# A reordered prologue in a sparse-attention and cosine-MLP kernel

## The chip, the cores and the metric

The kernel runs on one core of one Trainium2 chip. The metric is device time of one execution in microseconds (us). Engines: TensorE (PE, with its weight loads PEld), VectorE (DVE), ScalarE (ACT), GpSimd (POOL) and SyncE (SP), which here only issues transfers.

## The reference

```python
# q, k, v: (8 batches, 8 heads, 576 positions, 64)
scores = q @ k.T / sqrt(64)
mask_local   = (rel >= 0) & (rel < 32)                  # heads 0 to 3; rel = row - column
mask_strided = (rel >= 0) & (row % 32 == column % 32)   # heads 4 to 7
attn = softmax(where(mask, scores, -1e9)) @ v
x = attn, heads side by side                             # (4608 tokens, 512)
h = x @ w_in                                             # w_in: 512 x 2048
out = (h * cos(h)) @ w_out                               # w_out: 2048 x 512
```

The weights arrive as 64-bit floats, in pairs of 32-bit words, and the kernel makes float32 of them itself.

## The kernel before, in words

**Stages.** For each batch, attention gives x, transposed (features on partitions, 576 tokens in the free dimension). A first phase multiplies x by w_in and writes h to memory; a last phase reads h back, computes h*cos(h) and multiplies by w_out. Nearly all of this is matmuls on PE. Every large product is made of three: an operand is split into a high part (a cast, `x_hi` or `w` on ACT) and a remainder (a subtraction on POOL or DVE, `x_lo` and the second half of `w`), and PE adds high by high, high by low and low by high.

**Attention in units.** A batch has four strided units and three local ones. A unit loads q, k and v, gets its mask and its scores into a PSUM bank (L229, then L337 or L285), and goes through a softmax: DVE takes the maximum (L244) and subtracts it (L245), ACT makes the exponential (L250), DVE sums (L252), adds a tiny constant (L253) and takes the reciprocal (L254), POOL multiplies (L256). A strided unit is then turned by PE (L350), copied to SBUF by ACT (L354), multiplied by v (L363) and copied to x by ACT (L371, L377); once all four are there, x is split (`FirstOperands.split`, L155 on ACT and L156 on POOL, two halves of 288 tokens each). A local unit is turned by DVE (L293), multiplied by v (L303) and split straight from PSUM (L316 on ACT, L317 on DVE). So of the 512 features 256 are strided and 256 are local.

**Weights.** `land` brings 512 KB of w_in into one of three `raw` buffers; `to_float32` takes two operations of ACT (L142, L146) and two of DVE (L147, L150); `split` is a cast on ACT (L155) and a subtraction on POOL (L156). Two such pieces make the weights of one block `f` of 256 output columns; there are eight blocks.

**The prologue.** `PROLOGUE` says which unit takes its next step at which stage, and `BUSY` how many products of a zero tile (`keep_busy`, L630) PE makes after the scores of each stage. At stage 6 the conversion of the first two pieces of weights is put in, with the split of strided x. After the prologue comes the first batch, `FirstBlock`: eight products (L468) for each block, numbered n = 4*half + 2*rows + features, where features 0 are the strided ones and 1 the local ones. `FIRST` takes them in the order 0 to 7, so each PSUM bank gets its strided product and then its local one. Batch 1's scores and later attention work stand between these products, and the operations of all engines are placed by a scheduler that keeps each engine's queue in one fixed order, so an instruction waits for all that stand ahead of it on its engine.

**Later.** From batch 1 on a block has seven products of sums of operands (L497), for which POOL makes sums of weights (L182 to L192) and splits of x during the end of the first batch.

Of the kernel before, what the change touches and what calls it, by code (L numbers as in the profile page):

```python
# [26 lines left out]
P = 128  # L27
# [12 lines left out]
SU = 6  # L40
# [20 lines left out]
FIRST = ((0,), (1,), (2,), (3,), (4,), (5, 6), (7,))  # L61
PER_BATCH = NF * STEP
# [7 lines left out]
PROLOGUE = ((0,), (1,), (0, 2), (0, 1, 3), (1, 2, 4), (2, 3, 5), (3, 6), (4, 4), (5, 5), (6, 6))  # L70
BUSY = (10, 6, 5, 4, 4, 4, 4, 3, 3, 3)
# [9 lines left out]
def attention_cos_ffn(ctx, tc, qkl, vl, qkvs, w_in, w_out, eye, eye16, mask_l0, mask_l, mask_s, out):  # L81
# [15 lines left out]
    warm = const.tile([P, 64], BF16, name="warm")  # L97
# [101 lines left out]
    class Attention:  # L199
        def __init__(self, stack):  # L200
# [9 lines left out]
            self.kept, self.x = None, {}  # L210
# [7 lines left out]
        def pe(self, mm):  # L218
            return mm if self.plain else in_turn(mm)
# [5 lines left out]
        def score_bank(self, b, mask):  # L225
# [8 lines left out]
            if self.kept is None:  # L234
                self.kept = self.bank(self.scores)
                nc.vector.memset(self.kept, 0.0)
# [29 lines left out]
        def inputs(self, b, n):  # L266
            if b == 0:
                t = wp.tile([P, 6 * 2 * P], F32, name="v")
                return t[:, :n], t[:, n:]
            qk = self.ld.tile([P, max(QKL, QS + KS)], F32, name="qk")  # L270
            return qk, self.ld.tile([P, max(VL, VS)], F32, name="v")
# [53 lines left out]
        def strided(self, b, p, u):  # L325
            real = min(SU, NG - SU * u)
            qk, v = self.inputs(b, QS + KS)
            loads.append(nc.sync.dma_start(out=qk[:, :QS + KS], in_=qkvs[b, p, u, :, :QS + KS]))
# [16 lines left out]
            pn = next(self.pn_s)  # L345
# [106 lines left out]
    class FirstBlock:  # L452


        def __init__(self, f):
            self.f = f

        def products(self, slot):
            for n in FIRST[slot]:
                j, i, k = n // 4, n // 2 % 2, n % 2  # L460
                (wh, wl), (xh, xl) = wi[self.f][2 * i + k], operands[0].made[2 * k + j]
                if k == 0:
                    self.bank = pools["m"].tile([P, 512], F32, name="m")[:, :TH]
# [3 lines left out]
                for m, (a, y, c) in enumerate(ops):  # L467
                    in_turn(nc.tensor.matmul(  # L468
                        self.bank, a[:, c * P:(c + 1) * P], y[:, c], start=k == 0 and m == 0,
                        stop=k == 1 and m == len(ops) - 1, skip_group_check=True,  # L470
                    ))
                if k == 1:
                    h = getattr(self, f"h{i}")
                    if i:
                        nc.vector.tensor_copy(out=h[:, TH * j:TH * (j + 1)], in_=self.bank)
                    else:
                        nc.scalar.copy(out=h[:, TH * j:TH * (j + 1)], in_=self.bank)
# [124 lines left out]
    with ExitStack() as phase:  # L602
# [19 lines left out]
        att.banks(True, (m,), (o,), (acc[1], acc[2]), (m,))  # L622
# [5 lines left out]
        def keep_busy(n, after):  # L628
            for _ in range(n):
                mm = nc.tensor.matmul(  # L630
                    spare[:64], warm, warm.unsqueeze(1).broadcast_to([P, 8, 64]), start=True, stop=True
# [6 lines left out]
        for k, staged in enumerate(PROLOGUE):  # L638
# [4 lines left out]
            if k == 6:  # L643
                for i in range(2):
                    list(input_weights(cv, 0, i))
                operands[0].split(0)
# [178 lines left out]
```

## Time and profile before

| what | value |
|---|---|
| median of 3 runs | 890.8 us (887.82 to 892.25) |
| the profiled execution | 890.38 us, of which the span is 888.6 us |
| PE busy | 880.3 us, 99% of the span |
| DVE, ACT, POOL busy | 569.6, 531.0, 396.9 us |
| mean granted clock of PE | 0.995 |

The span is what the hardware profiler recorded, and 1.8 us of the execution lie around it. Matmuls are pipelined and overlap in the records, so PE reads as busy while it waits between small matmuls; the chain of waits and the start times say more than its busy share. A granted clock of 1.00 is 2.4 GHz, 0.50 is 1.2 GHz.

### The profile page before, as it was taken

The numbers are of one execution on the slowest core, as the hardware profiler recorded it, in microseconds if no ns is written. First come the engines' busy times: TensorE is split into PE (matmuls) and PEld (weight loads), VectorE is DVE, ScalarE is ACT, GpSimd is POOL, SyncE is SP. The second block draws the span as 40 slices with busy tenths as digits, with TensorE's granted clock in tenths as the row PEclk, the third lists the DMA queues.
The fourth block names the chain that finished last, engine by engine and source line by source line (L and its number), as shares of the span: only waits on it lengthen the run. The fifth ranks groups of instructions, "written<-read, shape, count | busy, mean of one in ns | idle before, by whom it ended". The sixth has DMA issues, their size and how long they took to land.

```text
span 888.6 us, 21381 instructions
## 1 busy us (share of the span) xinstructions
PE 880.3 (99%) x8453; PEld 780.9 (88%) x8453; DVE 569.6 (64%) x967; ACT 531.0 (60%) x1020; POOL 396.9 (45%) x337
## 2 busy tenths in 40 slices
PE   9999999999999999999999999999999999999998
PEld 5899999999999999999999888888888888888886
DVE  4788756757567676676425666666666666666662
ACT  3666544545345454454456777777777777777772
POOL 2568984415115051151455444444444444444442
PEclk9899999999999999999999999999999999999999
DMA  9488444565656556643285434343444344443431
GB/s 329 157 297 269 155 163 157 190 214 176 203 183 243 195 182 211 204 159 125 104 269 194 125 98 150 96 142 110 128 117 128 113 128 115 123 123 115 132 106 47
DMA packets 70516, 143.83 MB, mean 162 GB/s; under 512 B 8208, under 2 KB 15632, under 8 KB 70416
## 3 DMA queue, kind: packets, MB, share of 16 engines
q1 hardware_dynamic: 69696, 142.24, 50.0%
q8 instruction: 66, 1.08, 0.5%
q14 instruction: 34, 0.28, 0.1%
q10 hardware_dynamic: 720, 0.23, 0.1%
HBM read 91.06 MB, written 51.38 MB: 160 GB/s over the span
## 4 chain that ended last, share of the span: by engine, by line
PE 89%; POOL 3%; DVE 2%; DMA 2%; ACT 2%; issue 2%; SPq 0%; ACTq 0%; POOLq 0%
PE acc L588 45%; PE m L497 18%; PE n L497 9%; PE m L468 5%; PE o L497 4%; PE acc L303 2%; PE acc L285 2%; PE acc L363 2%; POOL x_lo L156 1%; PE acc L337 1%; DMA raw<-in_w_in 1%; PE acc L350 1%; DMA both<-w_all 1%; DMA v<-in_qkvs 0%; POOL v L156 0%
## 5 line engine op out<-in xcount | busy, mean ns | idle before, releaser
L156 POOL TENSOR_TENSOR g_lo<-r,g_hi 128x512 fp32r<-128x512 f32 x144 | 187.2, 1300 | 207.9 <-ACT g_hi L155 199.3
L588 PE MATMUL acc<-w,g_hi 128*128 128x512 f32 x720 | 223.1, 391 | 0.0
L577 DVE TENSOR_TENSOR r<-r,h_in 128x512 f32<-128x512 f32 x144 | 153.0, 1062 | 103.2 <-ACT r L573 103.1
L588 PEld LDWEIGHTS acc<-w,g_hi 128*128 128x128 f32 x720 | 135.3, 188 | 28.5
L588 PE MATMUL acc<-w,g_lo 128*128 128x512 f32 x360 | 141.1, 392 | 0.0
L571 ACT ACTIVATE r<-h_in 128x512 int32<-128x512 f32 x144 | 91.2, 633 | 80.5 <-POOL g_lo L156 80.3
L588 PE MATMUL acc<-v,g_hi 128*128 128x512 f32 x432 | 133.9, 391 | 0.0
L573 ACT ACTIVATE r<-r,quarter 128x512 f32<-128x512 f32 x144 | 104.3, 724 | 20.6 <-DVE r L572 15.9
L572 DVE SCALAR_TENSOR_TENSOR r<-r,h_in 128x512 f32<-128x512 int32 x144 | 101.7, 706 | 22.0 <-ACT r L571 13.2
L497 PE MATMUL m<-x_hi,w 128*128 128x288 f32 x448 | 109.8, 300 | 1.7 <-DVE h L515 1.6
L497 PE MATMUL m<-x_hi,v 128*128 128x288 f32 x448 | 108.9, 298 | 0.1
L588 PEld LDWEIGHTS acc<-v,g_hi 128*128 128x128 f32 x432 | 81.0, 188 | 17.2 <-ACT h L513 0.2
L155 ACT CAST g_hi<-r 128x512 fp32r<-128x512 f32 x144 | 89.6, 622 | 4.0 <-PE acc L588 1.8
L588 PE MATMUL acc<-v,g_lo 128*128 128x512 f32 x216 | 84.7, 392 | 0.0
L588 PEld LDWEIGHTS acc<-w,g_lo 128*128 128x128 f32 x360 | 67.6, 188 | 15.8
L497 PEld LDWEIGHTS m<-x_hi,w 128*128 128x128 f32 x448 | 78.0, 188 | 3.3 <-DVE h L515 2.4
L497 PEld LDWEIGHTS m<-x_hi,v 128*128 128x128 f32 x448 | 78.0, 188 | 1.2 <-ACT m L505 0.4
L505 ACT COPY m<-m 128x288 f32<-128x288 f32 x112 | 44.4, 397 | 55.2 <-PE m L497 51.1
L256 POOL TENSOR_TENSOR pn_s<-e_sb,z 128x324 f32<-128x324 f32 x32 | 23.3, 729 | 102.5 <-DVE z L254 77.8
L497 PE MATMUL m<-x_lo,w 128*128 128x288 f32 x224 | 66.1, 295 | 0.0
L497 PE MATMUL m<-x_lo,v 128*128 128x288 f32 x224 | 66.1, 295 | 0.0
L256 POOL TENSOR_TENSOR e_sb<-e_sb,z 128x384 f32<-128x384 f32 x24 | 20.4, 851 | 85.8 <-DVE z L254 76.2
(111 smaller groups left out, 1720.2 us busy)
## 6 DMA issues: line engine op xcount, KB each, us to landing
h_all<-h SPq DMA_DIRECT2D x128, 288.0 KB, 2.7
h_in<-h_all SPq DMA_DIRECT2D x144, 256.0 KB, 2.7
out<-o SPq DMA_DIRECT2D x36, 256.0 KB, 2.5
qk<-in_qkvs SPq DMA_DIRECT2D x28, 324.0 KB, 4.2
qk<-in_qkl SPq DMA_DIRECT2D x21, 416.0 KB, 4.0
raw<-in_w_in SPq DMA_DIRECT2D x16, 512.0 KB, 5.2
raw<-in_w_out SPq DMA_DIRECT2D x16, 512.0 KB, 4.5
v<-in_vl SPq DMA_DIRECT2D x24, 224.0 KB, 3.1
```

What stands on the lines that cost most here:

```text
L155: with_product(nc.scalar.copy(out=hi, in_=x))
L156: nc.gpsimd.tensor_tensor(out=lo, in0=x, in1=hi.bitcast(F32), op=ALU.subtract)
L256: nc.gpsimd.tensor_tensor(out=pn, in0=e, in1=z[:, :n].unsqueeze(2).broadcast_to([P, n, w]), op=ALU.mult)
L285: self.scored = self.pe(nc.tensor.matmul(s_ps[quarter_of(c), t * KW:(t + 1) * KW], q_t[half(j), p, QB * t:QB * (t + 1)], k_t[half(j), p, Q ...
L468: in_turn(nc.tensor.matmul(self.bank, a[:, c * P:(c + 1) * P], y[:, c], start=k == 0 and m == 0, stop=k == 1 and m == len(ops) - 1, skip_g ...
L497: in_turn(nc.tensor.matmul(bank, a[:, c * P:(c + 1) * P], y[:, c], start=first and i == 0, stop=i == len(ops) - 1, skip_group_check=True,))
L505: nc.scalar.copy(out=t, in_=self.bank[name[0]])
L571: with_product(nc.scalar.activation(out=k, in_=h, func=AF.Copy, scale=1.0 / (2.0 * math.pi), bias=0.25))
L572: nc.vector.scalar_tensor_tensor(out=r, in0=k, scalar=-2.0 * math.pi, in1=h, op0=ALU.mult, op1=ALU.add)
L573: sin = nc.scalar.activation(out=r, in_=r, func=AF.Sin, bias=quarter)
L577: nc.vector.tensor_tensor(out=r, in0=r, in1=h, op=ALU.mult)
L588: in_turn(nc.tensor.matmul(acc[t], g[:, at], w, start=(f == 0 and i == 0), stop=(f == NFC - 1 and i == 2)))
```

## The change

The edits: (1) in `PROLOGUE` the first step (scores and softmax) of each unit keeps its stage, and the later steps of the strided units come two stages later (those of the last one three and five), so that the local units' scores have less ahead of them; (2) `BUSY` now has 9 zero products at the start and 2 after each of six scores, 21 in place of 46, and each has 128 weight columns in place of 64; (3) weight conversion is put behind the scores of stage 6 (`turn = att.scored`), the split of strided x behind stage 9; (4) the four strided units of batch 0 no longer share the two `pn_s` tiles but write their probabilities into the unused end of their input tile, which POOL clears; (5) the second bank of a local unit's product comes from `acc0` and no longer from the three `m` banks; (6) the first block takes its eight products in the order of `VERY_FIRST`, three strided ones first, and keeps several banks open; (7) the scores' bank from batch 1 on is cleared by a zero product on PE and not by DVE.

```diff
@@ -59,6 +59,8 @@
 STEP = 7
 FIRST = ((0,), (1,), (2,), (3,), (4,), (5, 6), (7,))
+
+VERY_FIRST = ((0, 2), (4,), (1,), (3,), (5,), (6,), (7,))
 PER_BATCH = NF * STEP
 EXTRA = 2
@@ -67,8 +69,8 @@
 UNITS = 7
 KNOTS = ((UNITS, 1), (2 * UNITS + 2, PER_BATCH - 8), (B * UNITS + 2, (B - 1) * PER_BATCH - 8))
-PROLOGUE = ((0,), (1,), (0, 2), (0, 1, 3), (1, 2, 4), (2, 3, 5), (3, 6), (4, 4), (5, 5), (6, 6))
-BUSY = (10, 6, 5, 4, 4, 4, 4, 3, 3, 3)
+PROLOGUE = ((0,), (1,), (2,), (3,), (0, 4), (1, 0, 5), (2, 1, 6), (3, 2), (4, 4), (3,), (5, 5), (6, 6))
+BUSY = (9, 2, 2, 2, 2, 2, 2)
 TB = 512
 NTB = NTOK // TB
@@ -94,7 +96,7 @@
         nc.scalar.dma_start(out=t, in_=src)
     quarter = const.tile([P, 1], F32, name="quarter")
     nc.vector.memset(quarter, math.pi / 2.0)
-    warm = const.tile([P, 64], BF16, name="warm")
+    warm = const.tile([P, P], BF16, name="warm")
     nc.vector.memset(warm, 0.0)
     h_all = dram.tile([NFC, P, NTOK], F32, name="h_all")
     w_all = dram.tile([NFC, P, DM], F32, name="w_all")
@@ -207,7 +209,7 @@
             for t in pn_s:
                 nc.gpsimd.memset(t, 0.0)
             self.pn_s = itertools.cycle(pn_s)
-            self.kept, self.x = None, {}
+            self.kept, self.spare, self.x = None, None, {}
         def banks(self, plain, scores, transposed, products, second):
             self.plain = plain
@@ -216,6 +218,7 @@
             )
         def pe(self, mm):
+            self.last = mm
             return mm if self.plain else in_turn(mm)
         def bank(self, kind):
@@ -233,7 +236,9 @@
                 return bank
             if self.kept is None:
                 self.kept = self.bank(self.scores)
-                nc.vector.memset(self.kept, 0.0)
+                in_turn(nc.tensor.matmul(
+                    self.kept, warm, warm.unsqueeze(1).broadcast_to([P, 4, P]), start=True, stop=True
+                ))
             return self.kept
         def softmax(self, b, s, mask, n, w, pn=None):
@@ -266,6 +271,7 @@
         def inputs(self, b, n):
             if b == 0:
                 t = wp.tile([P, 6 * 2 * P], F32, name="v")
+                self.spare = t[:, 6 * 2 * P - SU * GP:].rearrange("p (t k) -> p t k", k=GP)
                 return t[:, :n], t[:, n:]
             qk = self.ld.tile([P, max(QKL, QS + KS)], F32, name="qk")
             return qk, self.ld.tile([P, max(VL, VS)], F32, name="v")
@@ -325,6 +331,7 @@
         def strided(self, b, p, u):
             real = min(SU, NG - SU * u)
             qk, v = self.inputs(b, QS + KS)
+            spare = self.spare
             loads.append(nc.sync.dma_start(out=qk[:, :QS + KS], in_=qkvs[b, p, u, :, :QS + KS]))
             nc.sync.dma_start(out=v[:, :real * D], in_=qkvs[b, p, u, :, QS + KS:QS + KS + real * D])
             q_t = qk[:, :QS].rearrange("p (t q) -> p t q", q=GB)
@@ -342,7 +349,11 @@
             yield [
                 partial(score, t, i) for t in range(SU) for i in range(2) if SU * u + t // 2 * 2 + i < NG
             ], "64x64"
-            pn = next(self.pn_s)
+            if b == 0:
+                pn = spare
+                nc.gpsimd.memset(pn, 0.0)
+            else:
+                pn = next(self.pn_s)
             self.softmax(b, s_ps[:, :SU * GB].rearrange("p (t w) -> p t w", w=GB), mask, SU, GB, pn[:, :, :GB])
             yield
             t_ps = self.bank(self.transposed)
@@ -453,28 +464,28 @@
         def __init__(self, f):
-            self.f = f
+            self.f, self.banks = f, {}
         def products(self, slot):
-            for n in FIRST[slot]:
+            for n in (FIRST if self.f else VERY_FIRST)[slot]:
                 j, i, k = n // 4, n // 2 % 2, n % 2
                 (wh, wl), (xh, xl) = wi[self.f][2 * i + k], operands[0].made[2 * k + j]
                 if k == 0:
-                    self.bank = pools["m"].tile([P, 512], F32, name="m")[:, :TH]
+                    self.banks[i, j] = pools["m"].tile([P, 512], F32, name="m")[:, :TH]
                     if j == 0:
                         setattr(self, f"h{i}", hb.tile([P, S], F32, name="h"))
                 ops = [(a, y, c) for c in range(2) for a, y in ((wh, xh), (wh, xl), (wl, xh))]
                 for m, (a, y, c) in enumerate(ops):
                     in_turn(nc.tensor.matmul(
-                        self.bank, a[:, c * P:(c + 1) * P], y[:, c], start=k == 0 and m == 0,
+                        self.banks[i, j], a[:, c * P:(c + 1) * P], y[:, c], start=k == 0 and m == 0,
                         stop=k == 1 and m == len(ops) - 1, skip_group_check=True,
                     ))
                 if k == 1:
                     h = getattr(self, f"h{i}")
                     if i:
-                        nc.vector.tensor_copy(out=h[:, TH * j:TH * (j + 1)], in_=self.bank)
+                        nc.vector.tensor_copy(out=h[:, TH * j:TH * (j + 1)], in_=self.banks[i, j])
                     else:
-                        nc.scalar.copy(out=h[:, TH * j:TH * (j + 1)], in_=self.bank)
+                        nc.scalar.copy(out=h[:, TH * j:TH * (j + 1)], in_=self.banks[i, j])
                     if j == 1:
                         nc.sync.dma_start(out=h_all[2 * self.f + i, :, :S], in_=h)
@@ -619,7 +630,7 @@
         att = Attention(attention)
         m, n, o = ((pools[name], name) for name in "mno")
         acc = [(ps, f"acc{i}") for i in range(3)]
-        att.banks(True, (m,), (o,), (acc[1], acc[2]), (m,))
+        att.banks(True, (m,), (o,), (acc[1], acc[2]), (acc[0],))
         operands[0] = FirstOperands()
         units = [unit for b in range(B) for unit in att.units(b)]
@@ -628,7 +639,7 @@
         def keep_busy(n, after):
             for _ in range(n):
                 mm = nc.tensor.matmul(
-                    spare[:64], warm, warm.unsqueeze(1).broadcast_to([P, 8, 64]), start=True, stop=True
+                    spare, warm, warm.unsqueeze(1).broadcast_to([P, 4, P]), start=True, stop=True
                 )
                 if after is not None:
                     order(mm, after, "in its place")
@@ -641,8 +652,11 @@
             if k + 1 < len(BUSY):
                 keep_busy(BUSY[k + 1], att.scored)
             if k == 6:
+                turn = att.scored
                 for i in range(2):
                     list(input_weights(cv, 0, i))
+            if k == 9:
+                turn = att.last
                 operands[0].split(0)
                 operands[0].split(1)
         for i in range(2):
```

**PE, where the products begin.** These rows are of PE around the scores of the first unit of batch 1 (`acc0_...<-qk`). `m_...` are the banks of the first block, `x_hi_119`, `x_hi_121` the two halves of strided x, `x_hi_123`, `x_hi_125` those of local x (`x_lo` likewise), `pt_l` the turned probabilities of a local unit. Before:

```order
L303 MATMUL m_574<-pt_l_469,v_430 64x32 x2
L468 MATMUL m_628<-x_hi_119,w_482 128x288
L468 MATMUL m_628<-x_lo_120,w_482 128x288
L468 MATMUL m_628<-x_hi_119,w_482 128x288 x2
L468 MATMUL m_628<-x_lo_120,w_482 128x288
L468 MATMUL m_628<-x_hi_119,w_482 128x288
L468 MATMUL m_628<-x_hi_123,w_482 128x288
L468 MATMUL m_628<-x_lo_124,w_482 128x288
L468 MATMUL m_628<-x_hi_123,w_482 128x288 x2
L468 MATMUL m_628<-x_lo_124,w_482 128x288
L468 MATMUL m_628<-x_hi_123,w_482 128x288
L337 MATMUL acc0_653<-qk_649 54x54 x12
```

After the change:

```order
L479 MATMUL m_629<-x_hi_121,w_434 128x288
L479 MATMUL m_629<-x_lo_122,w_434 128x288
L479 MATMUL m_629<-x_hi_121,w_434 128x288 x2
L479 MATMUL m_629<-x_lo_122,w_434 128x288
L309 MATMUL acc0_553<-pt_l_424,v_385 64x32 x2
L309 MATMUL acc0_553<-pt_l_424,v_385 64x64 x10
L309 MATMUL acc0_553<-pt_l_424,v_385 64x32 x2
L479 MATMUL m_629<-x_hi_121,w_434 128x288
L239 LDWEIGHTS warm_75
L239 MATMUL acc0_640<-warm_75 128x512
L344 MATMUL acc0_640<-qk_636 54x54 x12
L479 MATMUL m_607<-x_hi_123,w_434 128x288
```

Before, all products of the local units (L303) stand ahead of the first large product, and the first bank takes strided and local x in a row. In the changed kernel three products of strided x stand here, the last local unit's second product (L309) is inside the third of them, and local x is read only behind batch 1's first scores.

**ACT, the middle of the prologue.** `raw_...` to `n_...` and `w_...` are the steps of the weights, `e_sb` the exponential of a unit (324 wide strided, 384 local), `pt` and `x0` the copies of strided units. Before:

```order
L371 COPY x0_251<-acc1_238 128x6x18x3
L354 COPY pt_257<-o_253 128x324
L142 ACTIVATE n_477<-raw_474 128x512
L146 ACTIVATE raw_474<-raw_474 128x512
L146 ACTIVATE raw_485<-raw_485 128x512
L250 ACTIVATE e_sb_336<-e_sb_336 128x384
L371 COPY x0_251<-acc2_288 128x4x18x3
L377 COPY x0_251<-acc2_288 128x18x2
L155 CAST w_482<-v_476 128x512
L142 ACTIVATE n_487<-raw_485 128x512
L354 COPY pt_305<-o_301 128x324
L146 ACTIVATE raw_607<-raw_607 128x512
```

After the change:

```order
L255 ACTIVATE e_sb_352<-e_sb_352 128x384
L144 ACTIVATE n_429<-raw_426 128x512
L382 COPY x0_321<-acc2_372 128x4x18x3
L388 COPY x0_321<-acc2_372 128x18x2
L148 ACTIVATE raw_426<-raw_426 128x512
L148 ACTIVATE raw_437<-raw_437 128x512
L365 COPY pt_451<-o_447 128x324
L255 ACTIVATE e_sb_414<-e_sb_414 128x384
L382 COPY x0_321<-acc1_453 128x6x18x3
L157 CAST w_434<-v_428 128x512
L144 ACTIVATE n_439<-raw_437 128x512
L148 ACTIVATE raw_586<-raw_586 128x512
```

The first conversion (L142, now L144) stood behind the fourth unit's exponential and ahead of the first local unit's; now it stands behind the second local unit's.

**POOL, the splits.** `w_...` are the splits of weights, `x_lo_120` and `x_lo_122` those of strided x, `e_sb` the multiplication of the local units. Before:

```order
L156 TENSOR_TENSOR w_482<-v_476,w_482 128x512
L256 TENSOR_TENSOR e_sb_336<-e_sb_336,z_341 128x384
L156 TENSOR_TENSOR w_492<-v_476,w_492 128x512
L256 TENSOR_TENSOR e_sb_401<-e_sb_401,z_406 128x384
L156 TENSOR_TENSOR w_615<-v_609,w_615 128x512
L256 TENSOR_TENSOR e_sb_459<-e_sb_459,z_464 128x384
L156 TENSOR_TENSOR x_lo_120<-x0_251,x_hi_119 128x576
L156 TENSOR_TENSOR x_lo_122<-x0_251,x_hi_121 128x576
L156 TENSOR_TENSOR w_625<-v_609,w_625 128x512
L156 TENSOR_TENSOR w_699<-v_678,w_699 128x512
```

After the change:

```order
L261 TENSOR_TENSOR e_sb_288<-e_sb_288,z_293 128x384
L261 TENSOR_TENSOR e_sb_352<-e_sb_352,z_357 128x384
L158 TENSOR_TENSOR w_434<-v_428,w_434 128x512
L261 TENSOR_TENSOR e_sb_414<-e_sb_414,z_419 128x384
L158 TENSOR_TENSOR x_lo_120<-x0_321,x_hi_119 128x576
L158 TENSOR_TENSOR x_lo_122<-x0_321,x_hi_121 128x576
L158 TENSOR_TENSOR w_444<-v_428,w_444 128x512
L158 TENSOR_TENSOR w_594<-v_588,w_594 128x512
L158 TENSOR_TENSOR w_604<-v_588,w_604 128x512
L158 TENSOR_TENSOR w_685<-v_665,w_685 128x512
```

Before, three pieces of weights were split ahead of strided x; now one is, and the second piece, which the second product of the changed order reads, comes behind both splits of x.

## Rows read from the trace of the kernel before

**Rows 1.** The page, its first part (busy time, share of the span and instructions of each engine) and the granted clock in 40 slices of 22 us.

```profile
PE 880.3 (99%) x8453; PEld 780.9 (88%) x8453; DVE 569.6 (64%) x967; ACT 531.0 (60%) x1020; POOL 396.9 (45%) x337
...
PEclk9899999999999999999999999999999999999999
```

**Rows 2.** The chain that ended last, in order of time: start in us, length in us, what.

```profile
9.77 8.11 DMA raw<-in_w_in
...
29.80 1.20 PE acc L303 x28
...
34.12 3.18 PE m L468 x12
37.30 0.74 PE acc L337 x24
38.04 4.99 PE m L468 x36
```

**Rows 3.** Windows of 1 us: busy time of PE, PEld, DVE, ACT and POOL with instructions, granted clock, DMA share, GB/s.

```profile
30.00:31.00 1.00, 1.00 (x29) 0.94 (x26) 0.80 (x2) 1.00 (x3) 1.00 (x3) 0.73 0.58 229
31.00:32.00 1.00, 1.00 (x5) 0.19 (x6) 0.97 (x3) 1.00 (x5) 1.00 (x1) 0.50 0.30 45
...
37.00:38.00 1.00, 1.00 (x27) 0.71 (x25) 0.00 (x0) 0.67 (x2) 0.00 (x0) 0.86 0.00 0
38.00:39.00 1.00, 1.00 (x9) 1.00 (x8) 0.91 (x2) 0.85 (x2) 0.00 (x0) 1.00 0.06 16
```

**Rows 4.** Zero products: their group in the first 40 us (count, busy us, mean ns, idle before), from the view of groups by form.

```profile
L630 PE MATMUL acc<-warm 128*64 128x512 bf16 x46 | 14.2, 449 | 1.0 <-DVE warm L98 1.0
```

**Rows 5.** Zero products in the timeline of PE: start, length, line, count.

```profile
0.99 4.47 PE L630 MATMUL acc<-warm 128*64 128x512 bf16 x10 [0.99 <-DVE warm L98]
...
6.86 1.48 PE L630 MATMUL acc<-warm 128*64 128x512 bf16 x6
```

**Rows 6.** The timeline of DVE in the prologue: start, length, and in brackets the idle time ahead with what ended it.

```profile
6.98 0.49 DVE L244 TENSOR_REDUCE mx<-m 128x6 f32<-128x324 f32 x1 [6.04 <-PE m L337]
...
17.57 0.56 DVE L244 TENSOR_REDUCE mx<-m 128x6 f32<-128x384 f32 x1 [1.33 <-PE m L285]
...
28.92 0.19 DVE L254 RECIPROCAL z<-z 128x6 f32<-128x6 f32 x1
29.41 0.70 DVE L147 SCALAR_TENSOR_TENSOR n<-raw,n 128x512 int32<-128x512 int32 x1 [0.30 <-ACT n L142]
```

**Rows 7.** The timeline of ACT, same columns.

```profile
17.90 0.63 ACT L142 ACTIVATE n<-raw 128x512 int32<-128x512 uint32 x1 [0.39 <-DMA raw<-in_w_in]
18.47 1.40 ACT L146 ACTIVATE raw<-raw 128x512 f32<-128x512 f32 x2
...
20.18 0.35 ACT L371 COPY x<-acc 128x216 f32<-128x216 f32 x1
20.42 0.18 ACT L377 COPY x<-acc 128x36 f32<-128x36 f32 x1
...
22.02 0.68 ACT L146 ACTIVATE raw<-raw 128x512 f32<-128x512 f32 x1
22.98 0.52 ACT L250 ACTIVATE e_sb<-e_sb 128x384 f32<-128x384 f32 x1 [0.28 <-DVE e_sb L245]
23.57 0.62 ACT L155 CAST w<-v 128x512 fp32r<-128x512 f32 x1
24.09 0.64 ACT L142 ACTIVATE n<-raw 128x512 int32<-128x512 uint32 x1
24.66 0.48 ACT L371 COPY x<-acc 128x324 f32<-128x324 f32 x1
25.02 0.43 ACT L354 COPY pt<-o 128x324 f32<-128x324 f32 x1
...
29.78 1.25 ACT L155 CAST x_hi<-x 128x576 fp32r<-128x576 f32 x2
30.93 0.31 ACT L316 CAST x_hi<-acc 128x192 fp32r<-128x192 f32 x1
...
32.45 0.25 ACT L316 CAST x_hi<-acc 128x96 fp32r<-128x96 f32 x1
...
37.34 0.40 ACT L477 COPY h<-m 128x288 f32<-128x288 f32 x1 [1.49 <-PE m L468]
```

**Rows 8.** The timeline of POOL, same columns.

```profile
30.95 2.79 POOL L156 TENSOR_TENSOR x_lo<-x,x_hi 128x576 fp32r<-128x576 f32 x2
33.70 1.27 POOL L156 TENSOR_TENSOR w<-v,w 128x512 fp32r<-128x512 f32 x1
39.91 1.30 POOL L156 TENSOR_TENSOR w<-v,w 128x512 fp32r<-128x512 f32 x1 [4.94 <-ACT w L155]
```

**Rows 9.** Longer windows, columns as in rows 3.

```profile
40.00:60.00 20.00, 20.00 (x247) 19.29 (x245) 16.57 (x39) 13.23 (x28) 12.14 (x13) 1.00 0.85 280
60.00:80.00 20.00, 20.00 (x337) 19.00 (x339) 16.26 (x32) 13.70 (x30) 16.31 (x17) 1.00 0.83 262
80.00:95.00 15.00, 15.00 (x304) 14.38 (x297) 10.96 (x27) 7.75 (x18) 13.77 (x16) 1.00 0.74 256
95.00:112.00 17.00, 16.40 (x197) 15.71 (x197) 13.77 (x25) 8.82 (x21) 17.00 (x15) 1.00 0.42 137
```

**Rows 10.** DMA issues of the first 45 us by line: count, KB each, median us from issue to landing.

```profile
raw<-in_w_in SPq DMA_DIRECT2D x9, 512.0 KB, 5.3
```

## The prediction

> **What bounds the kernel now.** First the page's totals: PE is busy for 880.3 of the 888.6 us of the span [rows 1], so only what frees PE, or starts its large products sooner, moves the end. Then the chain of waits, in order of time: up to 34 us it runs through transfers, ACT and DVE, and from 34.12 on through the large products L468 without a gap (12 in 3.18 us, scores in 0.74, 36 in 4.99) [rows 2]. The order shows that PE's queue behind the first block's first 30 products is unchanged. So the change acts on the first 34 us, and the question is how much earlier PE gets through its first large products, and whether that lead survives. Third, the granted clock, us by us: PE falls from 2.4 to 1.2 GHz between 30 and 31 us, while small local products run, and is back at 2.4 between 37 and 38 [rows 3]. At the low level a large product takes 3.18/12 = 0.265 us, at the high one 4.99/36 = 0.139 [rows 2].
>
> A point that both kernels reach is needed. I take "18 large products and batch 1's first scores done". Before it is 38.04 + 6 x 0.139 = 38.87 us [rows 2].
>
> **The change part by part.**
>
> *Fewer zero products.* Before there are 46 with 14.2 us of busy time [rows 4], at 4.47/10 = 0.45 us on the low clock and 1.48/6 = 0.25 on the high one [rows 5]. 25 go: 1 x 0.45 + 24 x 0.25 = 6.4 us of PE. This is no gain in itself: DVE waits for PE only at times there (1.33 us ahead of the first local unit [rows 6]), and the head is set by what comes next. The 64 more weight columns I cost at nothing (a zero product streams 512 columns either way; at most its 0.25 again, twice per unit, in time that PE spends waiting).
>
> *Local softmax sooner, weights behind it.* DVE has to pass three times over each strided unit (0.49) and four times over each local one (0.56): 4 x 3 x 0.49 + 3 x 4 x 0.56 = 12.6 us, and 14 small operations of 0.19, 2.7: from 6.98 that ends at 22.3 if DVE never waits; before, the last reciprocal stood at 28.92 [rows 6], because conversions of weights stood in between and PE's scores came late. So DVE is no longer what is last; ACT is. Its order after the change can be added up from the arrival of the first piece of weights, which nothing in the change moves (its transfer ends the 8.11 us of [rows 2], and L142 starts at 17.90 [rows 7]). Up to the first `x_hi` of strided x stand, with durations from [rows 7]: L142 0.63, copies 0.35 + 0.18, L146 twice 1.40, copy of pt 0.43, exponential 0.52, copy of x 0.48, cast of w 0.62, L142 0.64, L146 0.68, two local `x_hi` 0.62, copies 0.35 + 0.18, and the cast itself 0.62: 7.70 us, so 25.6. Before, that cast ended at 29.78 + 0.62 = 30.4 [rows 7]. POOL then makes both `x_lo`, 2.79, and only then the low part of the second piece of weights, 1.27 [rows 8], which the third matmul of the second product reads: 29.7 us.
>
> Both sides of this: starts on ACT follow each other by about 0.1 less than the durations (23.57 to 24.09 for a cast of 0.62 [rows 7]), 13 times: 28.4 at the earliest. And ACT can be a microsecond late at the start, if DVE's share takes the 1.33 us of waiting that it had at 17.57 [rows 6]: 30.7 at the latest.
>
> *Strided products at the head.* From 29.7 on stand the last four matmuls of the second product and five of the third, up to the last local unit's second product: at the low clock 9 x 0.265 = 2.39, so 32.1. That local product also needs its bank back, thus the splits of the second local unit, which the new order puts behind conversions on ACT and DVE: after 25.6 ACT has the second `x_hi` 0.62, a cast 0.62, L142 0.64, L146 0.68, two small `x_hi` 0.50, a cast 0.62, L142 0.62, two more 0.50 = 4.80 [rows 7], so 30.4, and DVE in between two passes of 0.70 [rows 6] and a split of about 0.25: 32.1, the same. Then 1.20 for the local product at a falling clock (28 matmuls [rows 2]), 0.27 for the last of the 18, 0.45 for the zero product that replaces DVE's clearing, 0.74 for the scores: **34.8**, against 38.87: **4.1 us sooner**. The low end of the waits (1.3 less, all at the high clock, where the bank is the later one at 30.8) gives 30.8 + 0.6 + 0.14 + 0.25 + 0.74 = 32.5, 6.4 sooner. The high end (30.7 + 2.39 = 33.1, then 1.20, 0.27, 0.45 and the scores at half the clock, 1.48) gives 36.5, 2.4 sooner.
>
> *What is late next.* The seventh product needs the first bank, which ACT copies (0.40) only behind the last local splits and the conversions of two more pieces (0.31 + 0.64 + 0.68 + 0.64 + 0.68 + 0.62 + 0.40 = 3.97 [rows 7]); PE, from the same local product, needs 0.27 + 0.45 + 0.74 + 18 x 0.139 = 3.96. They meet; I cost this at 0, with 1 us as the far side. The two pieces have landed if a transfer takes its 5.3 us [rows 10] after the buffers come free at about 25 to 29.
>
> *The split of weights moved behind `x_lo`* costs POOL no new work: after 34.97 it idled 4.94 us before the change [rows 8]. The clearing of four input tiles lies before POOL's first use.
>
> *Whether the lead survives.* POOL is the narrow place later: it is busy for all 17.00 us from 95 to 112, while PE waits for its splits of batch 1 [rows 9]. To keep 4.1 us there POOL has to be that much ahead. From 40 to 95 it idles 7.86 + 3.69 + 1.23 = 12.8 us [rows 9], mostly waiting for ACT, which itself follows PE, and DMA is at 0.74 to 0.85. So most of the lead passes. In the last 15 us only 1.23 are idle, so some may not: I take 0.5, with 0 and all 4.1 as the ends.
>
> **Sum.** 890.38 (the profiled execution, span 888.6 and 1.8 around it) - 4.1 + 0.5 = **886.8 us**. The profiled execution is 0.4 below the median of the runs, so the same step from 890.8 would give 887.2.
>
> *The clock against the change.* The rows show the fall at 30 to 31 us with all 46 zero products in place [rows 3, 4]; with 25 fewer I expect it sooner, and the head is costed at 1.2 GHz for this. The Trainium skill, "TensorE: Matmul & The Clock Gate", section "Why this matters for your kernels", asks for matmul bursts without idle gaps, since PE falls back to its lower clock in them. By that rule the gaps that the new order leaves between the local units speak against the change, and it is one of the rivals, priced from rows below.
>
> **The rivals.**
>
> *All of it is gained* (chance 0.27). The starts on ACT follow each other as closely as in [rows 7], and the clock is back before the first scores: 6.4 sooner and no loss later, 884.0. For it: the spacing is in the trace. Against it: DVE and ACT hand work to each other at each conversion, and each hand-over adds.
>
> *The lead is lost later* (0.17). POOL, full from 95 to 112 us, does not begin sooner, because ACT and DVE (16.57 of 20 us busy) [rows 9] bring conversions no earlier: 0 to 1 sooner, 889.9. Against it: 12.8 us of idle POOL.
>
> *Slower: the clock stays low* (0.06). With zero products gone and the wait for the second piece of weights inside the head, PE is not granted 2.4 GHz until two blocks are through. The 30 other products of the first block and 48 of the second would cost 78 x (0.265 - 0.139) = 9.8 us: 890.4 - 4.1 + 9.8 = 896.1. It decides from 4.1/0.126 = 33 products on. Against it: before, the clock came back within 4 us of large products in a row [rows 2, 3].
>
> *The forecast* has 0.50, and between 885.2 and 888.8 as its own range.
>
> **How the numbers follow.** A measurement here can tell 0.5%, 4.4 us, from no change. The first rival lies beyond it, and of the forecast's range only its lowest part (gains over 4.4, 0.11 of the 0.50): faster 0.38. The rest of the forecast and the second rival are within it: 0.56. Slower 0.06. The range for 8 in 10 runs from 883.8, just under the first rival, to 890.2, past the second, and leaves the last one out.
>
> **What would show it.** In the profile after: about 21 zero products in place of 46; a first large product near 25.6 and a wait for POOL ahead of the second product's third matmul near 29.7; batch 1's first scores done near 35; the granted clock at 0.50 from before 27 to about 33; the first block's copy of a bank on ACT with no wait of PE on it; and POOL's full stretch beginning near 91 in place of 95. If scores of batch 1 end after 37, the sum of ACT is wrong; if they end near 35 and the total does not move, the loss lies at POOL or in the later batches; if L468's successors take 0.265 beyond 37 us, it is the clock.

## The result, and the profile after

| | before | after |
|---|---|---|
| median of 6 runs | 890.3 us (887.82 to 892.25) | 898.3 us (897.55 to 900.84) |
| the profiled execution | 890.38 us | 897.72 us |
| its span | 888.6 us | 895.9 us |
| mean granted clock | 0.995 | 0.993 |

The changed kernel is slower: ratio 1.0096, 95% interval 1.0075 to 1.0116, some 8 us. The prediction said 886.8 us, with 890.2 as the upper end.

The page after, its first part and the granted clock, against [rows 1]:

```profile
PE 883.5 (99%) x8429; PEld 779.8 (87%) x8429; DVE 575.8 (64%) x966; ACT 532.7 (59%) x1020; POOL 400.6 (45%) x341
...
PEclk9799999999999999999999999999999999999999
```

PE has 24 instructions fewer and is busy 3.2 us longer. Apart from the second slice the clock has not changed. So first the question of where along the span the time went. The first phase ends, and the second (L588 before, L599 after; unchanged code, the product of the gate with the output weights) begins, at the same place in both. The chain of waits (start, length, what, count) has that phase in one piece; below it stands a stretch of 40 us from its middle, the measure for all later runs. In the kernel before:

```profile
489.26 395.62 PE acc L588 x1728
...
599.90 40.28 PE acc L588 x176
```

and after:

```profile
488.95 403.27 PE acc L599 x1728
...
599.84 40.36 PE acc L599 x173
```

Up to the last phase the changed kernel is 0.31 us ahead. In the last phase PE waits for nothing in either kernel, and one product takes 40.28/176 = 0.2289 us before and 40.36/173 = 0.2333 after. The 1728 products take 403.27 - 395.62 = 7.65 us longer; less 0.3 that is 7.3, the whole difference of the spans. A stretch that the change does not touch, at the full clock, runs 1.9% slower.

**The first stage** came out as forecast on ACT and POOL, but not on PE. The timeline of PE after (start, length, line, shape, count; in brackets the idle time ahead and what ended it):

```profile
25.06 1.71 PE L309 MATMUL acc<-pt_l,v 32*64 32x32 f32 x28 [2.16 <-DVE x_lo L323]
26.70 0.61 PE L479 MATMUL m<-x_hi,w 128*128 128x288 f32 x1
27.23 2.84 PE L309 MATMUL acc<-pt_l,v 32*64 32x32 f32 x56
30.00 0.61 PE L479 MATMUL m<-x_lo,w 128*128 128x288 f32 x1
...
35.95 0.38 PE L239 MATMUL acc<-warm 128*128 128x512 bf16 x1 [0.48 <-DVE x_lo L323]
36.26 0.81 PE L344 MATMUL acc<-qk 64*54 64x54 f32 x24
37.00 0.40 PE L479 MATMUL m<-x_hi,w 128*128 128x288 f32 x1
```

ACT and POOL after, answering to [rows 7, 8]:

```profile
24.48 1.24 ACT L157 CAST x_hi<-x 128x576 fp32r<-128x576 f32 x2
...
25.23 2.80 POOL L158 TENSOR_TENSOR x_lo<-x,x_hi 128x576 fp32r<-128x576 f32 x2
27.97 2.52 POOL L158 TENSOR_TENSOR w<-v,w 128x512 fp32r<-128x512 f32 x2
```

"18 large products and batch 1's first scores done" is reached at 37.00 us, against 38.87 before: 1.9 us sooner. Windows after, columns as in [rows 3], show the clock around it:

```profile
22.00:24.00 2.00, 0.90 (x34) 0.70 (x24) 1.97 (x4) 2.00 (x7) 1.51 (x2) 0.98 0.62 220
24.00:26.00 2.00, 0.94 (x18) 0.94 (x20) 2.00 (x6) 1.97 (x6) 1.60 (x2) 0.50 0.29 113
...
32.00:34.00 2.00, 2.00 (x10) 1.86 (x8) 0.32 (x1) 0.00 (x0) 1.08 (x1) 0.50 0.75 256
34.00:36.00 2.00, 1.52 (x31) 1.17 (x30) 0.36 (x1) 0.81 (x3) 0.00 (x0) 0.96 0.02 6
```

PE is busy for less than half of the time from 22 to 26 us, and the clock is at 1.2 GHz from about 24 to 34.

**Where those 1.9 us go** shows in longer windows of PE alone (window, its length, busy time with products, granted clock, DMA share, GB/s), before:

```profile
100.00:118.00 18.00, 17.13 (x238) 1.00 0.41 145
118.00:330.00 212.00, 210.63 (x3095) 1.00 0.57 191
330.00:340.00 10.00, 10.00 (x151) 1.00 0.68 213
...
sum 451.00, PE 447.91; mean PE 89.58
```

and after:

```profile
100.00:118.00 18.00, 16.56 (x278) 1.00 0.41 140
118.00:330.00 212.00, 211.12 (x3080) 1.00 0.58 192
330.00:340.00 10.00, 8.63 (x99) 1.00 0.62 190
...
sum 451.00, PE 446.42; mean PE 89.28
```

From 38 to 489 us PE idles 451.00 - 447.91 = 3.09 us before and 451.00 - 446.42 = 4.58 after, 1.49 more: 0.57 more near 100 us, 1.37 near 335, 0.49 less in between. At the largest place PE stands at a product into bank `n` that ACT has not yet emptied:

```profile
335.51 0.40 PE L508 MATMUL n<-x_hi,v 128*128 128x288 f32 x1 [1.37 <-ACT n L516]
```

That copy begins at 335.07 after and at 334.62 before, behind an exponential for which ACT waits for DVE (its `e_sb` pass begins at 334.18 after, 333.73 before). There ACT and DVE do not run with PE's lead, and PE waits. (These are single executions. Of the kernels below, those with the order of before enter the last phase at 488.64 to 489.28 us, those with the whole new order at 487.16 to 488.75.)

### The profile page after: what moved, and what is told of

Read it like the earlier page. It is cut to its first block, busy times and chain, and to the rows that moved or that the text cites. A ratio compares the mean times of both kernels' runs of the same rounds, so it can differ in the third digit from the quotient of the medians.

```text
span 895.9 us, 21327 instructions
## 1 busy us (share of the span) xinstructions
PE 883.5 (99%) x8429; PEld 779.8 (87%) x8429; DVE 575.8 (64%) x966; ACT 532.7 (59%) x1020; POOL 400.6 (45%) x341
## 4 chain that ended last, share of the span: by engine, by line
PE 59%; DVE 2%; DMA 0%; issue 0%; ACT 0%; POOL 0%; DVEq 0%; POOLq 0%; ACTq 0%
PE acc L599 45%; PE m L508 7%; PE n L508 4%; PE o L508 2%; PE acc L309 1%; DMA h_all<-h 0%; PE acc L374 0%; DVE t L445 0%; PE acc L291 0%; DVE h L526 0%; PE acc L344 0%; DVE mx L253 0%; DVE z L257 0%; PE acc L361 0%; DVE acc L252 0%
## 5 line engine op out<-in xcount | busy, mean ns | idle before, releaser
L599 PE MATMUL acc<-w,g_hi 128*128 128x512 f32 x720 | 226.4, 396 | 0.0
L588 DVE TENSOR_TENSOR r<-r,h_in 128x512 f32<-128x512 f32 x144 | 159.5, 1108 | 102.8 <-ACT r L584 102.7
L599 PEld LDWEIGHTS acc<-w,g_hi 128*128 128x128 f32 x720 | 135.4, 188 | 32.6
L599 PE MATMUL acc<-w,g_lo 128*128 128x512 f32 x360 | 142.4, 396 | 0.0
L599 PE MATMUL acc<-v,g_hi 128*128 128x512 f32 x432 | 135.9, 396 | 0.0
L599 PEld LDWEIGHTS acc<-v,g_hi 128*128 128x128 f32 x432 | 81.1, 188 | 19.6 <-ACT h L524 0.2
L599 PE MATMUL acc<-v,g_lo 128*128 128x512 f32 x216 | 85.4, 396 | 0.0
L599 PEld LDWEIGHTS acc<-w,g_lo 128*128 128x128 f32 x360 | 67.7, 188 | 16.3
L261 POOL TENSOR_TENSOR pn_s<-e_sb,z 128x324 f32<-128x324 f32 x28 | 20.8, 741 | 92.3 <-DVE z L259 67.9
```

What stands on the lines that cost most here:

```text
L261: nc.gpsimd.tensor_tensor(out=pn, in0=e, in1=z[:, :n].unsqueeze(2).broadcast_to([P, n, w]), op=ALU.mult)
L588: nc.vector.tensor_tensor(out=r, in0=r, in1=h, op=ALU.mult)
L599: in_turn(nc.tensor.matmul(acc[t], g[:, at], w, start=(f == 0 and i == 0), stop=(f == NFC - 1 and i == 2)))
```

## Experiments

Two questions: what slows the unchanged last phase, and what the first stage's edits are worth alone.

In the compiled program, `warm` grew from 128 to 256 bytes a partition, and every tile that is allocated later on the left side of SBUF lies 128 bytes further. Among them are the output weights (`w`, `v`), which are the moving operand of the last phase's products, the one that streams through PE. Tiles on the right side have not moved; there lie the halves of the gate h*cos(h) (`g_hi`, `g_lo`), the stationary operand, which PE loads before it streams the other. The place theory makes this the cause. Its rival, the course theory: the new order of the first stage makes the other engines or the DMAs meet the last phase in another way.

**Moving tiles.** Four kernels, all timed against the kernel before. The first is the kernel before with a tile that nothing uses; the others have the same line with another size, or `warm` as it was.

```diff
     warm = const.tile([P, 64], BF16, name="warm")
     nc.vector.memset(warm, 0.0)
+    pad = const.tile([P, 64], BF16, name="pad")
+    nc.vector.memset(pad, 0.0)
```

> The kernel before with nothing but an unused tile of 128 bytes a partition allocated behind `warm`, so that every tile allocated later on the left side of SBUF, the output weights of the last phase among them, lies where the changed kernel has it. Place theory: the moving operand's address sets the pace of the 1728 products of L588/L599, so this kernel has the changed kernel's 0.2333 us for one in place of 0.2289, and 890.3 + 1728 x 0.0044 = 898 us. Course theory (the new order of the first stage makes other engines or the DMA meet the last phase differently): 0.2289 us for one and 890 us, because nothing in its order has changed.

Measured: 898.44 us, ratio 1.0099 (1.0079 to 1.0119); the first phase ends at 489.28 us, as in the kernel before, and in the last one

```profile
599.93 40.13 PE acc L590 x172
```

which is 0.2333 us for a product. An unused tile of 128 bytes gives the whole slowdown. The course theory falls.

```diff
-    warm = const.tile([P, P], BF16, name="warm")
+    warm = const.tile([P, 64], BF16, name="warm")
...
-                in_turn(nc.tensor.matmul(
-                    self.kept, warm, warm.unsqueeze(1).broadcast_to([P, 4, P]), start=True, stop=True
-                ))
+                nc.vector.memset(self.kept, 0.0)
...
-                    spare, warm, warm.unsqueeze(1).broadcast_to([P, 4, P]), start=True, stop=True
+                    spare[:64], warm, warm.unsqueeze(1).broadcast_to([P, 8, 64]), start=True, stop=True
```

> The changed kernel with `warm` back at 64 columns (its zero products again 64 by 512, the bank that is kept clear cleared by VectorE again), so that all tiles lie where the kernel before has them; the new order of the first stage stays. Place theory: 0.2289 us for a product of the last phase, and 898.3 - 7.6 = 890.7 us at most, 890.0 if the 0.3 us of lead at the last phase's start stays. Course theory: 0.2333 us and 898 us.

Measured: 890.85 us, ratio 1.0009 (0.9999 to 1.0019), 40.28 us for 176 products, 0.2289 each. The new order at the old places costs nothing in the last phase. (In the profiled execution, one of the longest of the ten at 892.36 us, that phase begins at 491.26, 2.0 us later than before. Why the head's lead is gone there comes up below; the rest of the 2.0 is open.)

The changed kernel with `pad` of 64 columns (128 bytes):

> The changed kernel with one more unused tile of 128 bytes a partition behind `warm`, so that later tiles lie 256 bytes on from where the kernel before has them. Place theory: the pace differs from one of the two seen if the period of the effect isn't 128 bytes; if the period is 256 bytes, 0.2289 us for a product and 890 us; if it is 512 or more, anything from 0.2267 (886.5 us) to 0.2333 (898 us). Course theory: 898 us.

Measured: 890.31 us, ratio 1.0001 (0.9991 to 1.0010), 0.2289 us for a product. So 256 bytes bring the old pace back.

The kernel before with `pad` of 16 columns (32 bytes):

> The kernel before with an unused tile of 32 bytes a partition behind `warm`: the output weights then begin at a multiple of 64 bytes, where both kernels so far have them 32 bytes behind one. Place theory: another pace than 0.2289 is possible, from 0.2267 (1728 x 0.0022 = 3.8 us less, 886.5 us) to 0.2333 (898 us); if the effect counts in steps of 64 bytes, 890 us. Course theory: 890 us.

Measured: 897.88 us, ratio 1.0086 (1.0067 to 1.0105), 40.13 us for 172 products, 0.2333 each. So it is no matter of multiples of 64 bytes: the weights begin at one here, and the pace is the slow one.

**A probe.** A kernel of such products alone; the places are byte offsets modulo 512 of the moving and the stationary operand. The edit is the whole body; its core:

```diff
+    def ops(m, s):
+        for k in range(2):
+            for t in range(NTT):
+                for i, (a, w) in enumerate(((0, 0), (0, 1), (1, 0))):
+                    g, y = s // 4 + 640 * a + t * P, m // 4 + 512 * w
+                    yield acc[t], sta[:, g:g + P], mov[:, y:y + 512], k == 0 and i == 0, k == 1 and i == 2
```

> Only the kind of product that fills the last phase: 128x128 stationary, 128x512 moving, both fp32r, 24 of them in the kernel's order for each of 36 pairs of places (the kernel's attention, its first product and its output are left out: zeros are written). L105 to L107 and the line with moving 288 and stationary 480 (bytes within 512, the kernel before's) repeat the known case. If the moving operand's place sets the pace: 24 x 0.2289 = 5.49 us at moving 32 and 288, 24 x 0.2333 = 5.60 us at 64, 160, 320 and 416, and no change while the stationary's place runs through its 16 values. If the distance between the two operands sets it: the pace changes with the stationary's place too, and is one and the same in the four lines that move both together. If it takes other engines' traffic: all lines at one pace. Some place may have 0.2267 us or less (5.44 us), which would be worth 3.8 us or more in the kernel.

(The lines called L105 to L107 there stand as L112 to L114 in the trace.) The chain of waits, a piece for each pair of places (start, length, line, count):

```profile
12.56 5.49 PE acc L113 x24
...
23.55 5.60 PE acc L115 x24
29.15 5.50 PE acc L116 x24
34.65 5.61 PE acc L117 x24
...
62.68 5.46 PE acc L122 x24
...
107.28 5.47 PE acc L130 x24
112.75 5.60 PE acc L131 x24
118.36 5.48 PE acc L132 x24
...
162.94 5.45 PE acc L140 x24
...
224.28 5.48 PE acc L151 x24
229.76 5.48 PE acc L152 x24
```

L115 to L130 run the moving operand from 0 to 480 in steps of 32, stationary at 480: only 32 (L116) and 288 on the one hand, 224 (L122) and 480 (L130) on the other are below 5.59. L131 to L146 run the stationary one from 0 to 480, moving at 288: now 32 (L132) and 288 (L140), 224 and 480 are below it. L151 and L152 have both at 0 and both at 64. So neither place decides by itself. It is the distance, moving less stationary, modulo 256 bytes: at 0 the 24 products take 5.45 to 5.48 us (0.227 to 0.228 each), at 64 5.49 to 5.51 (0.229 to 0.230), and at the other multiples of 32 5.59 to 5.62 (0.233 to 0.234). Four places off this grid (4, 8, 16 and 48 with 480) took 5.55 to 5.67 us. No other engine works during these products, and from 40 us on no transfer either, so the effect needs none. It also fits with the first phase's unchanged pace: there both operands lie on the left side and moved together by 128 bytes, so that their distances, 0 for half of the products and 128 for the other half, stayed as they were.

**Back in the kernel**, timed again: the kernel before with `pad` of 96 columns (192 bytes), the changed kernel with 32 columns (64 bytes), and the changed kernel with its left side as it is and the gate halves moved:

```diff
+    right = ctx.enter_context(tc.tile_pool(name="right", bufs=1, side="right"))
+    pad = right.tile([P, 32], BF16, name="pad")
+    nc.vector.memset(pad, 0.0)
```

> The kernel before with an unused tile of 192 bytes a partition behind `warm`: the output weights (moving) then lie a multiple of 256 bytes from the gate halves (stationary). Distance theory (in the probe the pace hangs on the distance of the two operands modulo 256 bytes: 0 gives 0.2267 us, 64 gives 0.2289, the others mostly 0.2333): 0.2267 us for a product of the last phase and 890.3 - 1728 x 0.0022 = 886.5 us. Theory of the moving operand's place alone (32 modulo 256 good, the others bad): 0.2333 us and 898 us.

> The changed kernel with an unused tile of 64 bytes a partition behind `warm`, so that its output weights too lie a multiple of 256 bytes from the gate halves. Distance theory: 0.2267 us for a product; 898.3 - 1728 x 0.0066 = 886.9 us, or 886.1 us if the 0.4 us that the first phase ends sooner shows. Moving operand's place alone: 898 us.

> The changed kernel with the left side as it is, output weights at 416 modulo 512 included, and an unused tile of 64 bytes a partition at the right end of SBUF, so that the gate halves go down from 480 to 416 modulo 512: distance 0. Distance theory: 0.2267 us for a product and 886.5 us. Moving operand's place alone: nothing that decides has changed, 0.2333 us and 898 us.

The chain in the middle of the last phase, in this order:

```profile
599.81 40.35 PE acc L590 x178
```

```profile
599.96 40.12 PE acc L601 x177
```

```profile
599.92 40.12 PE acc L602 x177
```

All kernels side by side (places modulo 256; the time per product from the chain):

| kernel | weights | gate halves | distance | us per product | median us | ratio to before |
|---|---|---|---|---|---|---|
| before | 32 | 224 | 64 | 0.2289 | 890.3 | |
| after | 160 | 224 | 192 | 0.2333 | 898.3 | 1.0096 |
| before, moved 128 | 160 | 224 | 192 | 0.2333 | 898.4 | 1.0099 |
| before, moved 32 | 64 | 224 | 96 | 0.2333 | 897.9 | 1.0086 |
| after, moved back | 32 | 224 | 64 | 0.2289 | 890.9 | 1.0009 |
| after, moved 256 in all | 32 | 224 | 64 | 0.2289 | 890.3 | 1.0001 |
| before, moved 192 | 224 | 224 | 0 | 0.2267 | 886.4 | 0.9960 (0.9943 to 0.9977) |
| after, moved 192 in all | 224 | 224 | 0 | 0.2267 | 885.8 | 0.9959 (0.9944 to 0.9974) |
| after, gate halves moved | 160 | 160 | 0 | 0.2267 | 885.9 | 0.9968 (0.9951 to 0.9985) |

The ratios of the last three rows are to executions of the kernel before beside them, with a median of 889.8 us. In the last row the weights lie where the slow kernel has them, and the pace is the best one. The three kernels with distance 0 beat both kernels of this case.

**The first stage's edits.** Read from one profiled execution each, on the changed kernel moved by 256 bytes, whose own figures are: scores of batch 1 begin at 36.09 us, last phase at 488.75 us, span 888.1 us. First, the bank of batch 1's scores cleared by VectorE again (edit 7 undone):

> The changed kernel with later tiles 256 bytes on (as in the run that had 890.31 us) and one hunk undone: the bank that is kept clear is cleared by VectorE again, not by a zero product. If that product is what keeps the clock up between the local products and batch 1's first scores, PE shows a wait of over 1 us there and the clock goes back to 0.50 near 38 us, and the large products at 50 us are 1.9 us later than with it; if the 64 columns of the zero products did that in the run where both were undone, nothing changes here.

The scores, and the clock around them:

```profile
37.17 0.81 PE L344 MATMUL acc<-qk 64*54 64x54 f32 x24 [1.20 <-issue]
```

```profile
36.00:38.00 2.00, 0.83 (x25) 1.00 0.00 0
38.00:40.00 2.00, 2.00 (x10) 0.60 0.45 130
40.00:45.00 5.00, 5.00 (x47) 0.82 0.78 273
```

As the first half of the expectation says: PE idles over 1 us, then the clock is back at the low level for a while. Its second half holds too: batch 1's first turn on PE (L350 before, at 51.19 us) begins at 51.84, 2.6 later than with the zero product (49.25). Of this 0.7 lies ahead of the gap (the 18th large product starts at 35.57 against 34.91), which leaves 1.9. The run with both hunks undone (above) had the same 1.20 us, 0.50 from 38 to 40 us, and that turn at 51.10. So without this one zero product the head's lead over the kernel before is gone by 50 us in both executions. The last phase begins at 490.17 us here, span 889.5, but the next run begins it as late with the zero product in place. The prediction cited the Trainium skill, "TensorE: Matmul & The Clock Gate", section "Why this matters for your kernels", on idle gaps and the lower clock; this trace agrees in that the clock fell behind a gap, at the place where a zero product had closed it, though the gap, 1.20 us, is shorter than those the section warns of.

Second, the zero products' width alone:

> The changed kernel with later tiles 256 bytes on and one hunk undone: the zero products go back to 64 weight columns (8 x 64 moving). If their width is what the clock looks to, it falls from 1.00 sooner than near 26 us or rises later than near 33 us, and the large products at 50 us come later than with 128 columns; if not, lead at 50 us 1.9 us and span about 888 us as in the run with 256 bytes.

The clock falls as after (0.95 from 20 to 25 us against 0.89, then 0.50 up to 34 in both) and rises a little later (0.80 against 0.96 from 34 to 36); scores at 36.56, last phase from 490.16, span 889.5. Against the kernel moved by 256 bytes the clock is lower for longer (that one had 1.00 from 20 to 25 us, 0.63 from 25 to 30, 0.71 from 32 to 34), but that kernel and the changed one, both with wide zero products, differ from each other as much. This is inconclusive: 0.5 us at the scores is too little to lay to the width by one execution, and the 1.4 us at the end of the first phase are more than that and were not foreseen.

Third, 16 more zero products:

> The changed kernel with later tiles 256 bytes on and the counts of zero products of the kernel before in their first seven places (10, 6, 5, 4, 4, 4, 4 in place of 9, 2, 2, 2, 2, 2, 2: 16 more). If the lead of the first stage came out at 1.9 us and not 4.1 because 16 large products and the local products ahead of them ran at 1.2 GHz, a clock that stays at 1.00 there takes half of 16 x 0.24 + 2.36 = 6.2 us, up to 3.1 us, off: batch 1's first scores near 33 us in place of 36. If the large products are held by x_lo and the weights' low part, the scores stay near 36 us; if the zero products stand in the way of the local units, they come later than 36. The time in all: within 1 us of 890.3 in each case if the rest of the first phase takes the lead back as it did.

Scores at 36.86 us, last phase from 489.64, span 889.0: the third answer. The clock holds longer (0.76 over 25 to 30 us against 0.63) but is still at 0.50 from 30 to 34, and the local product that begins at 26.48 has waited 2.39 us for DVE. One execution shows no more than that the zero products did not bring the scores forward.

**Whose weights count.** Last, whether a product meets its own stationary operand or the next one's:

> Products alone again (the kernel's attention, its first product and its output are left out, zeros are written), to see which stationary operand counts. L118 to L120: both operands at one place modulo 256, 24 x 0.2267 = 5.44 us. L121, L122: 128 bytes apart, 5.60 us. L123, L124: places alternate between 0 and 128 from product to product, each product's own two operands at one place, the next product's stationary 128 bytes from this moving operand. L125, L126: the same alternation, but each product's own operands 128 bytes apart and the next one's stationary at this moving operand's place. If a product's own two operands count: 5.44 us at L123 and 5.60 at L125. If it is the weights of the next product, loaded while this one streams: 5.60 at L123 and 5.44 at L125. L129 to L136: 288 columns (the first phase's size) at distances 0 to 224 in steps of 32: 24 x 0.1333 = 3.20 us at 0 if the first phase's pace is the best one, and up to 24 x 0.0067 = 0.16 us more at others. L137 to L144: bf16, 512 columns: one pace if the effect belongs to four-byte operands.

```profile
14.94 5.44 PE acc L119 x24
...
31.41 5.60 PE acc L122 x24
37.01 5.48 PE acc L123 x24
...
47.98 5.52 PE acc L125 x24
...
70.13 3.16 PE acc L129 x24
73.28 3.20 PE acc L130 x24
...
79.65 3.16 PE acc L132 x24
82.81 3.20 PE acc L133 x24
...
95.59 5.20 PE acc L137 x24
...
105.97 5.18 PE acc L139 x24
```

Neither: both alternations lie between 5.44 and 5.60, so this stays open. It also bounds the reading above: the distance within each product sets the pace where all products of a stream have the same one, but in L125 each product's own operands are 128 bytes apart, and it is faster than L122. With 288 columns the effect is one of 3.16 to 3.20 us and falls otherwise: distances 0, 64 and 96 take 3.16, the others 3.19 or 3.20. In bf16 distance 0, the first line, takes 5.20 us and the seven others 5.18, so 0 brings no gain there.

## Why the prediction was wrong

- **The step that failed** is "The 64 more weight columns I cost at nothing". The zero products themselves cost nothing that the runs show. But the wider `warm` moved all later tiles on one side, and the prediction priced no effect of that on the last 400 us: +7.6 us, shown by the unused tile alone. None of its rivals held this; the one on the slower side ("the clock stays low") did not occur, as the clock is at 0.96 from 34 to 36 us.
- **Large products at the head, 4.1 us sooner: 1.9 measured.** ACT's sum (25.6; the first of two casts in 1.24 us from 24.48 ends near 25.1) and POOL's (29.7; the first of two splits in 2.52 us from 27.97 ends near 29.2) were right to 0.5 us, but PE did not wait for them: the wait for POOL near 29.7 did not come. What failed is "9 x 0.265". PE had waited 2.16 us, up to 25.06, for DVE's split of local x, which the prediction did not price, and then only one large product ran before local products took PE for 2.84 us. So 16 were left from 30.00 on up to the last local product, 16 x 0.24 at the low clock (14 start in the 3.36 us from 30.41) in place of 2.39 us: 1.5 of the 2.2 us that are missing. Ahead of the bank's clearing came a wait of 0.48. The prediction's own sign for this, that scores ending after 37 us would make the sum of ACT wrong, would have misled: they end at 37.0, and that sum held.
- **25 fewer zero products, no gain in itself:** right as far as the runs go; 21 are left, and with 16 given back the scores came at 36.86 us in place of 36.09, one execution each.
- **Whether the lead survives (0.5 lost):** wrong in size and place. Of 1.9 us 1.6 are lost by 489 us, and not to POOL: near 100 and 335 us PE waits for banks that ACT and DVE empty. At equal places the whole change but for its moving of tiles is worth nothing measurable: ratio 1.0001 (0.9991 to 1.0010). The median of that kernel, 890.3 us, is near the time of the rival "the lead is lost later" (889.9 us), but by another mechanism. That the forecast's gain is missing would thus stand even without the moved tiles.
- **The clock low from before 27 to about 33:** right (24 to 34).

## What to carry over

A change of a tile's size moves every tile allocated behind it: when an untouched stretch changes its pace at full clock and without waits, compare the addresses before the schedules, and test with an unused tile of the same size. For a long stream of products like those of the last phase (fp32r, the four-byte format of the large products, with 512 columns), try the moving and the stationary tile at the same place modulo 256 bytes; here that was worth 0.4%, more than the whole reordering. A lead won in a prologue has to be followed to the end: here most of it went where PE waited for banks that ACT and DVE empty.

## What the runs showed of the hardware

In streams with one distance throughout, at the full clock, a product of 128x128 by 128x512 in fp32r took 0.2267, 0.2289 or 0.2333 us in the kernels, and the distance between its two operands modulo 256 bytes set which (0, 64, or another multiple of 32); in bf16 it took 5.18/24 to 5.20/24, 0.216 to 0.217 us, at all eight distances. The Trainium skill, "SBUF — State Buffer", section "A bandwidth-pool intuition that's wrong (but worth ruling out)", gives TensorE's weight loads a second, independent read port. The bf16 lines are in line with it, 5.18 to 5.20 us whatever the distance; for fp32r an independent port alone gives no reason for the distance to count, and the measurement decides. Why the chip behaves so, no run here shows.
